# Splitting the row threshold into three f16 parts: subtractions on TensorE instead of VectorE

## The chip, the cores and the metric

The kernel runs on one core of a Trainium2 chip. The metric is the device time of one execution in microseconds (us), as the median over several runs. Engines are TensorE (PE, its weight loads apart as PEld), VectorE (DVE), ScalarE (ACT), GpSimd (POOL) and SyncE (SP, which here issues DMAs).

## What is computed

Masked attention over 8 batches of 8 heads, then a mixture of experts that takes one expert for each token:

```python
scores = scale * np.matmul(q, k.transpose(0, 1, 3, 2))          # q, k, v: (8, 8, 576, 64)
thresh = np.max(scores, axis=-1, keepdims=True) - tau
scores = np.where(scores >= thresh, scores, -1000000000.0)
scores = scores - np.max(scores, axis=-1, keepdims=True)
attn = np.exp(scores)
attn = attn / (np.sum(attn, axis=-1, keepdims=True) + 1e-09)
x = np.matmul(attn, v)                  # then laid out as (4608, 512)
logits = x @ w_gate                     # 8 experts
expert_idx = np.argmax(logits, axis=1)
...
    h = np.maximum(xe @ w1[e], 0.0)     # w1[e]: 512 x 1024
    ye = h @ w2[e]
    out[mask] = gate_w[mask, None] * ye
```

## The kernel before

The kernel treats the heads as 32 pairs. Queries, keys, values and weights are held as two f16 parts (high and low), so that products in f16 reach the accuracy that is wanted. A pair takes eleven steps, and each step works on one tile of up to 128 x 512 scores.

Each pair goes through the scores twice. The first pass (`s_unit`, L312 and L314 on TensorE) computes scores `s` with queries as rows, and VectorE takes the negated maximum of each row (`nm`, L324). The second pass (`st_unit`, L360 and L361) computes them again transposed (`st`), with the threshold already subtracted: the rows 64 to 66 of the tile `CQ` hold, for each query, minus its row's maximum plus a multiple of tau, and the product L361 adds them to the scores by three rows of ones. ScalarE then takes the exponential (`e`, L377), VectorE zeroes what lies below the threshold (`e`, L380), ScalarE rounds to f16 (`ph`, L385) and GpSimd makes the rest (`pl`, L386). TensorE multiplies both with the values (`av`, L422 to L424). The first pass runs ten steps ahead of the second.

Since `CQ` is f16, the threshold is split into three f16 parts. This is `parts`: VectorE takes the minimum of the two halves of the row maxima (`r`, L331), TensorE transposes it (`pst`, L335) into 9 x 128 elements of a PSUM tile, and then a chain of four operations makes the three parts `ptT`: ScalarE rounds value plus threshold (L340), VectorE subtracts the rounded part from value plus threshold and writes the rest beside it in PSUM (`y`, L341), ScalarE rounds the rest (L342), VectorE subtracts again and writes the third part as f16 (L343). Three DMAs on SyncE's queue bring the parts into `CQ` (`rows`, L348).

The helper `chain` spreads such operations over steps: element i of a list goes to the step k + i // 2, alternately to the middle and to the end of a step. The PSUM tile of `pst` comes from a pool of one buffer with the tag `m`, which the logits (`lg`, L494), the ranks (`rk`, L539 to L542) and the counts use as well. 

Other work between: a high part of queries and keys (`hi`, ScalarE L230) is multiplied by a unit matrix into PSUM (`hi`, TensorE L244), and VectorE makes the low part from it (`lo`, L245). The values go the same way (`vop` on ScalarE L276, `hi_v` on TensorE L244, `vop` on VectorE L245). When a batch is done (four pairs), its logits, its choice of experts and the ranks of its tokens are computed, and GpSimd scatters the tokens' rows to DRAM by expert (L560, `xs`), after it scaled them (`xn`, L465). Towards the end of attention the experts' weights are loaded (`wf`, L717) and split into two f16 parts (`wb`, ScalarE L730 and VectorE L731); tokens are gathered (L764), transposed by DMA (L774 for gathered tokens, L480 for those of the logits) and multiplied (`h`, L819, and `y`, L852). Two of the first token slots lie in a tile `spare`.

The order on each engine isn't the order of the code alone: the framework builds the program with its own list scheduler, which orders all instructions by a model of their times. An edit at one place can so move instructions at others.

Of the kernel before, what the change touches and what calls it, by code (L numbers as in the profile page):

```python
# [9 lines left out]
F16 = mybir.dt.float16  # L10
# [3 lines left out]
AF = mybir.ActivationFunctionType  # L14
ALU = mybir.AluOpType
AX = mybir.AxisListType

P = 128
# [32 lines left out]
def kernel(  # L51
# [9 lines left out]
    nc = tc.nc  # L61

    cpool = ctx.enter_context(tc.tile_pool(name="cpool", bufs=1))
# [19 lines left out]
    ident = cpool.tile([P, P], F32, name="ident")  # L83
    make_identity(nc, ident)
    ident_h = cpool.tile([P, P], F16, name="ident_h")
    nc.gpsimd.tensor_copy(ident_h, ident)
    ones = cpool.tile([P, P], F16, name="ones")
    nc.gpsimd.memset(ones, 1.0)
    before = cpool.tile([P, P], F16, name="before")
# [3 lines left out]
    thr = cpool.tile([P, 1], F32, name="thr")  # L93
# [95 lines left out]
    def after(k, f, where=END):  # L189
        plan(now[0] + k, f, where)  # L190

    def chain(k, fs, at_once=False):

        if at_once:
            for f in fs:
                after(k, f, END)
            return
        for i, f in enumerate(fs):
            i += slot[0] > FRONT and k == 0
            after(k + i // 2, f, END if i % 2 else MID)  # L200
# [125 lines left out]
    def parts(n):  # L326


        nm = st[n]["nm"]
        r = small.tile([P, 9], F32, tag="r", name=f"r_{n}")  # L330
        nc.vector.tensor_reduce(r, nm.rearrange("p a t -> p t a"), axis=AX.X, op=ALU.min)  # L331

        def turn():
            ps = ps_m.tile([P, 512], F32, tag="m", name=f"pst_{n}")
            nc.tensor.transpose(ps[0:9, 0:P], r, ident)  # L335
            x, y = ps[0:9, 0:P], ps[0:9, P:2 * P]
            t = small.tile([9, 3, P], F16, tag="ptT", name=f"ptT_{n}", bufs=1)
            v, a = nc.vector, nc.scalar
            chain(1, [
                lambda: a.activation(t[:, 0], x, AF.Identity, bias=thr[0:9]),  # L340
                lambda: v.scalar_tensor_tensor(y, x, thr[0:9], t[:, 0], ALU.add, ALU.subtract),  # L341
                lambda: a.copy(t[:, 1], y),  # L342
                lambda: (v.tensor_tensor(t[:, 2], y, t[:, 1], ALU.subtract), rows(t)),  # L343
            ])

        def rows(t):
            for p in range(3):
                nc.sync.dma_start(  # L348
                    st[n]["CQ"][64 + p:65 + p].rearrange("p (t c) -> p t c", t=9), t[:, p]
                )  # L350

        after(1, turn)
# [714 lines left out]
    if True:  # L1067
# [9 lines left out]
        while busy:  # L1077
# [3 lines left out]
            for z in (("st", "s"), ("s", "st"))[TUNE["ord"]]:  # L1081
                n, t = divmod(k + (NSTEP + LEAD if z == "s" else 0), NSTEP)
# [11 lines left out]
            n, t = divmod(k - TUNE["av"], NSTEP)  # L1094
# [95 lines left out]
```

## Time and profile before

| | |
|---|---|
| median of three runs | 1040.5 us (1040.37 to 1044.72) |
| the profiled execution | 1042.02 us |
| its span (first to last instruction) | 1040.3 us |
| mean granted clock of TensorE | 0.976 |
| TensorE busy | 958.2 us, 92% |
| VectorE busy | 719.1 us, 69% |
| ScalarE busy | 653.1 us, 63% |
| GpSimd busy | 556.3 us, 53% |

A row of the profile names a line of the kernel, an engine, an operation and, after it, the tile that it writes and those that it reads; "x32" is a count, and a time in brackets with an arrow is the idle time of the engine just before and what ended it. Attention fills the span to about 620 us, the experts the rest; pairs begin every 16 to 17 us, but for six that take about 22.

### The profile page before, as it was taken

Reading aid. Unit: us, or ns where it says so; the run is one execution under the profiler, and the core shown is the slowest. Engines: PE = TensorE matmul, PEld = TensorE weight load, DVE = VectorE, ACT = ScalarE, POOL = GpSimd, SP = SyncE. Lnnn points to the kernel's source line nnn. Section 1 sums busy time; section 2 is a strip of 40 time slices with the busy share of each in tenths; the row PEclk is TensorE's granted clock in tenths of the full one; section 3 lists DMA queues with packets and bytes.
Section 4 is the critical chain, followed back from the end, with each engine's and each line's share of the span. In section 5 each row is a group of like instructions: output and inputs, shape, how many; then the busy total and the mean of one; then the engine's idle time right before and its main releaser. Section 6 shows DMA issues by size and latency. Waiting matters only on the chain.

```text
span 1040.3 us, 28272 instructions
## 1 busy us (share of the span) xinstructions
PE 958.2 (92%) x11336; PEld 622.9 (60%) x11336; DVE 719.1 (69%) x1443; ACT 653.1 (63%) x1098; POOL 556.3 (53%) x460
## 2 busy tenths in 40 slices
PE   2799998999898998998996689999999999999996
PEld 1365655566464665564663476767766676667683
DVE  6999998899797997997998964664332433423650
ACT  2588998888787987987977773524342433433641
POOL 3266887976977967968867773153221222122121
PEclk9999999899999999999998898999999999999998
DMA  6534554754465645546534536989746746556720
GB/s 185 140 92 110 138 131 116 164 122 116 132 156 144 134 102 155 139 105 180 127 87 134 140 84 214 310 266 236 231 142 172 232 132 178 170 156 217 225 82 25
DMA packets 142562, 159.16 MB, mean 153 GB/s; under 512 B 96345, under 2 KB 112731, under 8 KB 142428
## 3 DMA queue, kind: packets, MB, share of 16 engines
q1 hardware_dynamic: 126796, 100.35, 37.7%
q10 hardware_dynamic: 6480, 27.53, 8.9%
q0 software_dynamic: 9152, 29.45, 8.7%
q8 instruction: 90, 1.47, 0.6%
q14 instruction: 44, 0.36, 0.1%
HBM read 90.24 MB, written 19.44 MB: 105 GB/s over the span
## 4 chain that ended last, share of the span: by engine, by line
PE 50%; DVE 7%; issue 6%; DMA 4%; ACT 3%; POOL 1%; another core or an unknown queue 1%; POOLq 0%; ACTq 0%; DVEq 0%; SPq 0%
PE h L819 16%; PE y L852 14%; PE st L360 3%; PE s L312 3%; PE s L314 3%; PE st L361 3%; PE av L422 2%; DMA out_dram<-o,gt 2%; DVE wb L731 2%; PE av L423 2%; PE av L424 2%; DVE e L380 2%; DVE nm L324 1%; DMA wf<-in_w_dram 1%
## 5 line engine op out<-in xcount | busy, mean ns | idle before, releaser
L386 POOL TENSOR_TENSOR pl<-e,ph 128x1024 f16<-128x1024 f32 x158 | 336.8, 2142 | 144.2 <-ACT ph L385 103.2
L377 ACT ACTIVATE e<-st,ntau 128x512 f32<-128x512 f32 (+1 forms) x352 | 223.1, 653 | 65.5 <-PE st L361 36.2
L324 DVE TENSOR_REDUCE nm<-s 128x1 f32<-128x512 f32 x320 | 200.4, 633 | 39.9 <-PE s L314 26.0
L380 DVE SCALAR_TENSOR_TENSOR e<-st,e 128x512 f32<-128x512 f32 (+1 forms) x352 | 219.8, 635 | 5.4 <-ACT e L377 4.6
L852 PE MATMUL y<-wb,hl 128*128 128x512 f16 (+1 forms) x1056 | 203.6, 362 | 1.1 <-issue 0.7
L819 PEld LDWEIGHTS <-wb 128*128 128x128 f16 x2304 | 190.4, 99 | 23.3 <-issue 4.9
L819 PE MATMUL h<-xTm,wb 128*128 128x256 f16 (+2 forms) x2112 | 198.0, 255 | 3.1 <-issue 3.1
L422 PE MATMUL av<-vop,ph 128*128 128x65 f16 (+1 forms) x1536 | 186.3, 195 | 4.7 <-issue 2.5
L424 PE MATMUL av<-vop,ph 128*128 128x64 f16 (+1 forms) x1536 | 185.7, 196 | 2.3 <-issue 2.3
L423 PE MATMUL av<-vop,pl 128*128 128x65 f16 (+1 forms) x1536 | 184.8, 194 | 3.2 <-issue 2.9
L385 ACT CAST ph<-e 128x1024 f16<-128x1024 f32 x160 | 166.8, 1043 | 18.6 <-DVE e L380 18.3
L422 PEld LDWEIGHTS <-ph 128*128 128x128 f16 (+1 forms) x1536 | 148.8, 101 | 31.5 <-issue 11.9
L423 PEld LDWEIGHTS <-pl 128*128 128x128 f16 (+1 forms) x1536 | 148.6, 100 | 29.1 <-issue 12.3
L312 PE MATMUL s<-QK 128*128 128x512 f16 (+3 forms) x640 | 141.4, 299 | 24.7 <-DMA QK<-lo 17.3
L424 PEld LDWEIGHTS <-ph 128*128 128x128 f16 (+1 forms) x1536 | 148.7, 100 | 24.7 <-issue 11.5
L731 DVE SCALAR_TENSOR_TENSOR wb<-wf,wb 128x1024 f16<-128x1024 f32 x96 | 125.2, 1341 | 49.1 <-ACT wb L730 45.7
L852 PEld LDWEIGHTS <-hl 128*128 128x128 f16 (+1 forms) x1056 | 94.5, 100 | 101.3 <-issue 6.3
L360 PE MATMUL st<-QK 128*128 128x512 f16 (+3 forms) x640 | 142.4, 298 | 8.8 <-DVE e L380 5.3
L361 PE MATMUL st<-CQ,ck 128*128 128x512 f16 (+3 forms) x640 | 139.7, 293 | 0.7 <-DMA CQ<-hi 0.4
L314 PE MATMUL s<-ck,CQ 128*128 128x512 f16 (+3 forms) x640 | 137.8, 292 | 1.2 <-DMA CQ<-hi 1.2
L864 POOL DMA_INDIRECT out_dram<-o,gt x40 | 44.4, 1111 | 143.9 <-ACT o L863 127.1
L807 ACT ACTIVATE hl<-h 128x512 f16<-128x512 f32 (+1 forms) x80 | 45.8, 573 | 113.6 <-PE h L819 106.7
(182 smaller groups left out, 1092.8 us busy)
## 6 DMA issues: line engine op xcount, KB each, us to landing
wf<-in_w_dram SPq DMA_DIRECT2D x96, 512.0 KB
qkf<-in_qk_dram ACTq DMA_DIRECT2D x30, 576.0 KB
vf<-in_v_dram ACTq DMA_DIRECT2D x15, 640.0 KB
QK<-hi SPq DMA_DIRECT2D x64, 144.0 KB
QK<-hi SPq DMA_DIRECT2D x64, 72.0 KB
QK<-lo SPq DMA_DIRECT2D x64, 72.0 KB
ck<-lo SPq DMA_DIRECT2D x64, 72.0 KB
CQ<-hi SPq DMA_DIRECT2D x64, 64.0 KB
```

Of the source, the lines that this page charges most:

```text
L312: nc.tensor.matmul(sc[rows, oc], d["QA"][a][:, cols], d["KB"][a][:, CH[c]], start=True, stop=False)
L324: nc.vector.tensor_reduce(o, sc[:, 0:width(t)], axis=AX.X, op=ALU.max, negate=True)
L360: nc.tensor.matmul(sc[rows, oc], d["KB"][a][:, cols], d["QA"][a][:, CH[c]], start=True, stop=False)
L361: nc.tensor.matmul(sc[rows, oc], d["CK"][a][:, cols], d["CQ"][:, q], start=False, stop=True)
L377: nc.scalar.activation(pf, sc, AF.Exp, bias=ntau, scale=0.125 / SS)
L380: nc.vector.scalar_tensor_tensor(pf, sc, 0.0, pf, ALU.is_ge, ALU.mult)
L386: (nc.vector if (n, t) in PLV else nc.gpsimd).tensor_tensor(l, pd, h, ALU.subtract)
L422: nc.tensor.matmul(av, h, vop[:, tv, 0:W], start=i in (0, NT) and m == 0, stop=False)
L423: nc.tensor.matmul(av, l, vop[:, tv, 0:W], start=False, stop=False)
L424: nc.tensor.matmul(av[:, 0:D], h, vop[:, tv, W:W + D], start=False, stop=last)
L819: nc.tensor.matmul(o, Wt[:, c, wh, f], x, start=c == 0 and z == 0, stop=c == 3 and z == 2,)
L852: nc.tensor.matmul(o, h[:, hh], Wt[:, f, wh, c], start=f == 0 and z == 0, stop=f == 7 and z == 2)
```

## The change

A constant `minus` (9 x 9, f16, minus the unit matrix) is made once. The rest `y` is no longer written beside the value. Instead TensorE subtracts the rounded part from the value in PSUM: a product of `minus` and the part, accumulated on what `pst` left there. ScalarE makes all three parts with the same operation, which adds the threshold and rounds. The chain has five elements now instead of four.

```diff
+    minus = cpool.tile([9, 9], F16, name="minus")
+    nc.vector.tensor_scalar(minus, ident[0:9, 0:9], -1.0, None, ALU.mult)
...
-            nc.tensor.transpose(ps[0:9, 0:P], r, ident)
-            x, y = ps[0:9, 0:P], ps[0:9, P:2 * P]
+            nc.tensor.matmul(ps[0:9, 0:P], r, ident, start=True, stop=True, is_transpose=True)
+            x = ps[0:9, 0:P]
             t = small.tile([9, 3, P], F16, tag="ptT", name=f"ptT_{n}", bufs=1)
-            v, a = nc.vector, nc.scalar
+
+            def part(p):
+                nc.scalar.activation(t[:, p], x, AF.Identity, bias=thr[0:9])
+
+            def less(p):
+                nc.tensor.matmul(x, minus, t[:, p], start=False, stop=True, skip_group_check=True)
+
             chain(1, [
-                lambda: a.activation(t[:, 0], x, AF.Identity, bias=thr[0:9]),
-                lambda: v.scalar_tensor_tensor(y, x, thr[0:9], t[:, 0], ALU.add, ALU.subtract),
-                lambda: a.copy(t[:, 1], y),
-                lambda: (v.tensor_tensor(t[:, 2], y, t[:, 1], ALU.subtract), rows(t)),
+                lambda: part(0), lambda: less(0), lambda: part(1), lambda: less(1), lambda: (part(2), rows(t)),
             ])
```

In the changed kernel the roundings have the line L343, the subtractions L346, `pst` L337; lines further down are higher by six.

The scheduler orders the changed program anew. Three places follow; names carry the pair, then the tile where there is one, then a running number, so `st_20_3` is tile 3 of pair 20.

The first place is the chain of pair 21. TensorE before:

```order
L244 MATMUL hi_23_2_8198<-hi_23_8145,ident_h_99 128x384
L335 MATMUL pst_21_8150<-ident_94,r_21_8127 9x128
L422 LDWEIGHTS ph_19_8_7800
L422 MATMUL av_19_1_8391<-vop_1_166,ph_19_8_7800 128x65
L423 LDWEIGHTS pl_19_8_7801
L423 MATMUL av_19_1_8391<-vop_1_166,pl_19_8_7801 128x65
L424 LDWEIGHTS ph_19_8_7800
L424 MATMUL av_19_1_8391<-vop_1_166,ph_19_8_7800 128x64
```

TensorE in the changed kernel, at the same place:

```order
L246 MATMUL hi_23_2_8221<-hi_23_8168,ident_h_99 128x384
L337 MATMUL pst_21_8173<-ident_94,r_21_8150 9x128
L430 LDWEIGHTS ph_19_8_7819
L430 MATMUL av_19_0_8197<-vop_1_168,ph_19_8_7819 64x64
L346 LDWEIGHTS minus_101
L346 MATMUL pst_21_8173<-ptT_21_8175,minus_101 9x128
L246 LDWEIGHTS ident_h_99
L246 MATMUL hi_v10_1_0_8225<-vop_0_167,ident_h_99 128x320
```

One product stands between `pst` and the first subtraction, and a `hi_v` product, which needs `vop`, follows at once; before, products of `av` followed `pst`. ScalarE at this place before:

```order
L377 ACTIVATE e_20_2_8156<-st_20_3_8190,ntau_107 128x512
L430 COPY x_4_7117<-av_19_0_8174 128x4x65
L431 COPY xh_4_7116<-av_19_0_8174 64x65
L526 COPY was_4_9422<-run_151 128x8
L340 ACTIVATE ptT_21_8152<-pst_21_8150,thr_105 9x128
L276 ACTIVATE vop_0_165<-vf_10_7535 128x10x64
L211 DMA qkf_25_8538<-in_qk_dram 128x1152
L342 CAST ptT_21_8152<-pst_21_8150 9x128
L385 CAST ph_20_2_8157<-e_20_2_8156 128x1024
```

ScalarE in the changed kernel:

```order
L532 COPY was_4_9445<-run_153 128x8
L383 ACTIVATE e_20_2_8179<-st_20_3_8213,ntau_109 128x512
L343 ACTIVATE ptT_21_8175<-pst_21_8173,thr_107 9x128
L278 ACTIVATE vop_0_167<-vf_10_7557 128x10x64
L436 COPY x_4_7138<-av_19_0_8197 128x4x65
L437 COPY xh_4_7137<-av_19_0_8197 64x65
L343 ACTIVATE ptT_21_8175<-pst_21_8173,thr_107 9x128
L213 DMA qkf_25_8562<-in_qk_dram 128x1152
```

The first part and `vop` now stand ahead of the copies `x` and `xh`, and the second part behind them.

The second place is GpSimd's scatter of batch 3 (`xs`, five of them in one row), in pair 20. Before:

```order
L386 TENSOR_TENSOR plc_20_10_8306<-e_20_10_8304,phc_20_10_8305 128x64
L386 TENSOR_TENSOR pl_20_8_8260<-e_20_8_8258,ph_20_8_8259 128x1024
L560 DMA xs_81<-R_197,posi_3_7978 36864x514 x5
L465 TENSOR_TENSOR xn_4_0_8576<-x_4_7117,rs_4_8520 128x512
L465 TENSOR_TENSOR xn_4_1_8755<-x_4_7117,rs_4_8520 128x512
L386 TENSOR_TENSOR pl_20_4_8381<-e_20_4_8379,ph_20_4_8380 128x1024
L386 TENSOR_TENSOR pl_20_6_8438<-e_20_6_8436,ph_20_6_8437 128x1024
```

In the changed kernel:

```order
L392 TENSOR_TENSOR plc_20_10_8330<-e_20_10_8328,phc_20_10_8329 128x64
L392 TENSOR_TENSOR pl_20_8_8280<-e_20_8_8278,ph_20_8_8279 128x1024
L392 TENSOR_TENSOR pl_20_4_8405<-e_20_4_8403,ph_20_4_8404 128x1024
L566 DMA xs_81<-R_199,posi_3_8001 36864x514 x5
L471 TENSOR_TENSOR xn_4_0_8600<-x_4_7138,rs_4_8544 128x512
L471 TENSOR_TENSOR xn_4_1_8780<-x_4_7138,rs_4_8544 128x512
L392 TENSOR_TENSOR pl_20_6_8462<-e_20_6_8460,ph_20_6_8461 128x1024
```

One `pl` has moved ahead of the scatters.

The third place is SyncE's queue where the experts begin (`xTg` and `xTm` are transposed tokens, `wf` weights). Before:

```order
L717 DMA wf_2_0_0_13271<-in_w12_dram 128x1024
L774 DMA_TRANSPOSE spare_13173<-spare_13173 128x8x128
L717 DMA wf_2_1_0_13314<-in_w12_dram 128x1024
L717 DMA wf_1_3_0_13347<-in_w12_dram 128x1024
L717 DMA wf_2_0_1_13363<-in_w12_dram 128x1024
L480 DMA_TRANSPOSE xTg_7_0_13226<-R_197 128x8x128
L774 DMA_TRANSPOSE spare_13173<-spare_13173 128x8x128
L480 DMA_TRANSPOSE xTg_7_0_13226<-R_197 128x8x128
```

In the changed kernel, where five loads and a transpose stand between `wf_2_0_0` and the first row here:

```order
L486 DMA_TRANSPOSE xTg_7_0_13260<-R_199 128x8x128
L723 DMA wf_2_1_1_13578<-in_w12_dram 128x1024
L723 DMA wf_1_1_1_13589<-in_w12_dram 128x1024
L486 DMA_TRANSPOSE xTg_7_2_13279<-R_199 128x8x128
L723 DMA wf_2_3_0_13593<-in_w12_dram 128x1024
L486 DMA_TRANSPOSE xTg_7_2_13279<-R_199 128x8x128
L486 DMA_TRANSPOSE xTg_7_4_13290<-R_199 128x8x128
L780 DMA_TRANSPOSE spare_13207<-spare_13207 128x8x128
```

Both transposes of `spare` now come behind those of the last batch's tokens.

## The prediction

> **What bounds the kernel now.** I read the page first (its chain of waits, by engine), then cut the attention part into stretches by the view of windows, and then asked in each stretch which engine waits for which.
>
> ```profile
> PE 50%; DVE 7%; issue 6%; DMA 4%; ACT 3%; POOL 1%; another core or an unknown queue 1%; POOLq 0%; ACTq 0%; DVEq 0%; SPq 0%
> ```
>
> TensorE has half of the chain that ended last, VectorE 7%. That is a mean over stages, so the next view is one of stages: the start, four plain pairs (9 to 12), the pair that begins at 403.8, the last two pairs with the first weight splits, and a window of the MoE part. Behind a stretch and its length stand the busy us (and instructions) of TensorE, its weight loads, VectorE, ScalarE and POOL, then TensorE's granted clock.
>
> ```profile
> 26.00:51.20 25.20, 19.66 (x129) 8.23 (x130) 23.18 (x48) 13.09 (x23) 5.17 (x4) 0.93 0.52 142
> 191.20:257.00 65.80, 65.29 (x985) 40.57 (x983) 61.71 (x134) 56.36 (x104) 49.48 (x32) 1.00 0.55 125
> 403.80:426.10 22.30, 18.95 (x236) 11.07 (x235) 16.78 (x34) 16.39 (x29) 20.53 (x17) 0.92 0.42 128
> 549.00:600.00 51.00, 32.83 (x431) 20.85 (x431) 46.10 (x69) 35.78 (x58) 38.35 (x28) 0.87 0.49 128
> 640.00:660.00 20.00, 20.00 (x239) 14.29 (x238) 11.51 (x15) 10.73 (x16) 8.59 (x8) 0.96 1.11 292
> ```
>
> In the four plain pairs both TensorE (65.29 of 65.8 us) and VectorE (61.71) look full, so busy time can't decide; the waits can. First TensorE's and VectorE's in 191.2 to 257, then TensorE's in 549 to 600 (us in total, times, longest):
>
> ```profile
> PE pst L335 <- DVE r L331: 0.4, 1, 0.4
> DVE nm L324 <- PE s L314: 2.9, 8, 0.7
> PE st L360 <- DVE e L380: 5.0, 2, 2.7
> PE s L312 <- DVE e L380: 4.3, 1, 4.3
> ```
>
> In plain pairs TensorE waits for nothing but once 0.4 us, while VectorE waits eight times for TensorE: **TensorE is the bound there**, VectorE a close second with 65.8 − 61.7 = 4.1 us to spare in four pairs. At the end of attention it is the other way round, TensorE waits over 9 us for VectorE. In the pair at 403.8 POOL is the fullest, and TensorE has 3.4 us idle. In the MoE part TensorE is full again, and the change has no instruction there.
>
> **The change part by part.** The tile views give each operation's minimum, median and maximum in ns:
>
> ```profile
> L340 ACT ACTIVATE ptT<-pst,thr x32: 342/354/359, 29.6 to 585.6; 9x128 f16<-9x128 f32 x32
> L341 DVE SCALAR_TENSOR_TENSOR pst<-pst,thr,ptT x32: 337/341/347, 32.0 to 591.0; 9x128 f32<-9x128 f32 x32
> L342 ACT CAST ptT<-pst x32: 233/250/256, 32.4 to 592.0; 9x128 f16<-9x128 f32 x32
> L343 DVE TENSOR_TENSOR ptT<-pst,ptT x32: 268/269/279, 32.7 to 593.5; 9x128 f16<-9x128 f32 x32
> ```
>
> *VectorE.* 32 × (341 + 269) = 19.5 us go, 0.61 in a pair. In plain pairs this lies beside a full TensorE and is worth nothing. It is worth something where TensorE waits for VectorE: chains 29 to 31 in the last stretch, whose 46.1 busy us fill most of 51, 2 × 0.61 = 1.2 us there (the third chain's share falls into VectorE's wait for weights). And at the start:
>
> ```profile
> 32.40 0.26 ACT L342 CAST ptT<-pst 9x128 f16<-9x128 f32 x1 [2.42 <-DVE pst L341]
> 32.56 0.74 ACT L276 ACTIVATE vop<-vf 128x640 f16<-128x640 f32 x1
> ...
> 33.36 0.44 PE L244 MATMUL hi_v<-vop,ident_h 128*128 128x320 f16 x2 [3.77 <-ACT vop L276]
> ```
>
> L341 stands behind VectorE's queue there, ScalarE waits 2.42 us for it with `vop` behind, and TensorE waits 3.77 us for `vop`. Without VectorE in the chain this 2.42 goes; late next are VectorE's own low parts and maxima (23.18 busy of 25.2), so I count 1.4 (between 0.61, one chain's work, and 2.42). Together −2.6 (bounds 0 and −19.5).
>
> *ScalarE.* 32 more roundings of 354 ns, and 32 × (354 − 250) for the ones that were casts: 14.7 us, 0.46 in a pair. The cover is its slack: 65.8 − 56.4 = 9.4 us in four pairs, 2.4 in one. Counted as nothing; with the cover gone it would be 14.7.
>
> *TensorE.* 64 products of 9x128. No such row exists; the nearest are the 512-column products, which start 0.21 apart, and `pst` itself, the same 128 columns in f32, whose follower starts 0.11 later (the last row is for the waits below):
>
> ```profile
> 210.78 0.28 PE L335 MATMUL pst<-ident,r 128*9 128x128 f32 x1 [0.38 <-DVE r L331]
> 210.89 0.19 PE L423 MATMUL av<-vop,pl 128*128 128x65 f16 x1
> ...
> 212.00 0.38 PE L360 MATMUL st<-QK 128*128 128x512 f16 x1
> 212.21 0.38 PE L361 MATMUL st<-CQ,ck 128*128 128x512 f16 x1
> 212.25 0.36 ACT L340 ACTIVATE ptT<-pst,thr 9x128 f16<-9x128 f32 x1
> ```
>
> A quarter of 0.21 is 0.054: 64 × 0.054 = 3.5 us, or 7.0 by the other row. Below, nothing, if they all fall into waits that are there anyway. I take 3.5, since the new products are f16 like the 512-column ones.
>
> *New waits on TensorE.* Each first subtraction waits for ScalarE's first part, each second one for the second, and behind them in TensorE's order stand products of other pairs that need neither. The order puts from 0 to 3.9 us of other products between `pst` and the first subtraction, and 1.2 to 3.8 between the two. That is enough in most pairs: ScalarE's part 0 followed `pst` by 1.47 us and took 0.36 in pair 11, where 2.1 us of products now stand between. In pair 21 hardly one product is left between them, and the `hi_v` products follow directly:
>
> ```profile
> 393.17 0.27 PE L335 MATMUL pst<-ident,r 128*9 128x128 f32 x1
> ...
> 393.49 0.36 ACT L340 ACTIVATE ptT<-pst,thr 9x128 f16<-9x128 f32 x1
> ...
> 393.75 0.73 ACT L276 ACTIVATE vop<-vf 128x640 f16<-128x640 f32 x1
> ```
>
> Part 0 ends at 393.85, `vop` at 394.48, and TensorE has only till about 393.3 to do: 0.6 us of wait for the subtraction, then some 0.7 for `hi_v`, 1.3 in all. The same arithmetic with each pair's rows gives 0.4 to 2.0 us in eight more pairs and almost nothing in the others, 7.7 in sum. Pairs 9, 17 and 25 cost nothing: TensorE waits there for `vop` anyway, behind the same L340.
>
> ```profile
> PE hi_v L244 <- ACT vop L276: 3.3, 3, 1.5
> PE hi_v L244 <- ACT ptT L340: 3.0, 1, 3.0
> ```
>
> Three of the waits (pairs 14, 21, 29: 2.9 us) lie close ahead of or in a stretch where TensorE idles for POOL. So I take 5. Bounds: 0, if these waits are all taken back there, and 13, if in each of the 26 pairs without a long idle time the rounding's 0.36 us and the two hand-overs around it (0.5) stand open.
>
> *`m` and the rows.* The one buffer of `m` is held until the last rounding, a half step longer; its next users are the logits and ranks, several steps on. The three row transfers leave a half step later, seven steps before `st` of that pair reads them. I count nothing: a late transfer would show as a wait of L361 for `CQ`, and the lists of waits above have none.
>
> *POOL's order.* In the pair at 403.8 five scatters, the last of them the first row here, and two `xn` stand ahead of `pl`:
>
> ```profile
> 409.68 0.96 POOL L560 DMA_INDIRECT xs<-R,posi  x1 [0.30 <-issue]
> 410.67 2.04 POOL L465 TENSOR_TENSOR xn<-x,rs 128x512 f32<-128x512 f32 x2
> 412.67 2.12 POOL L386 TENSOR_TENSOR pl<-e,ph 128x1024 f16<-128x1024 f32 x1
> ```
>
> In three such blocks one `pl` now stands ahead of the scatters or of the two `xn`. That can shorten TensorE's idle time by up to one `pl` (2.1) each, −6, or only move it; it can also push the scatters back, +2. I take −1.
>
> *Start of the MoE part.* On SyncE the transposes of the two spare slots move behind some nine more transfers and transposes, and TensorE takes other products first. TensorE is full there now (20.00 of 20.0 us from 640), and its products on the spare slots run from 653.4:
>
> ```profile
> L819 PE MATMUL h<-spare,wb x192: 216/219/220, 653.4 to 670.2; 128*128 128x128 f16 x192
> L774 SPq DMA_TRANSPOSE spare<-spare x2: 2587/2934/3282, 637.4 to 645.3; - x2
> ```
>
> A second transpose at 645.3 with nine entries more ahead (0.7 to 3 us each) comes some 13 us later, and other products have to fill that. I take +1; bounds +6, if only half of these 13 us find other products, and −3, if the other order fills waits that stand ahead of 640.
>
> **The sum.** The profiled execution took 1042.0 us (span 1040.3 and 1.7 around it): 1042.0 + 3.5 + 5 − 2.6 − 1 + 1 = 1047.9. It lies 1.5 above the median of the three runs, so on their scale 1046.4, rounded 1046.5, which is 0.6% slower.
>
> **Rivals.** *A, VectorE is the bound.* For it: 61.71 of 65.8 us busy, and the end and start wait for it. Against: it waits for TensorE 2.9 us in four pairs, TensorE for it 0.4. If each pair shortened by its 0.61: 1040.5 − 19.5 = 1021, with the subtractions up to 1031. The Trainium skill, Perfetto Trace Analysis, section Identifying the Most-Contended Engine, says that a matmul's busy share misjudges TensorE and that the engine with the highest occupancy is to be relieved first. By that rule VectorE (94% of these pairs against 62% for weight loads) would be the one, and this rival true. The waits of this trace speak against it.
>
> *B, the order comes out better.* Six pairs of the trace are as long as that at 403.8, 22.3 us instead of 65.8 / 4 = 16.5, so some 34 us are there to be had. If the three POOL blocks give 2.1 each, the waits nothing, and the rest is as above: 1042.0 + 3.5 − 2.6 − 6.3 + 1 − 1.5 = 1036, with a spread of 1030 to 1041. For it: the rows of the order. Against: POOL has 20.53 of 22.3 us to do in that pair whatever the order.
>
> *C, slower: the new waits halve the clock.* After idle times of TensorE the granted clock falls to a half for 3.4 us:
>
> ```profile
> 324.80:326.40 1.60, 0.08 (x2) 0.04 (x1) 0.35 (x1) 1.52 (x7) 1.60 (x1) 1.00 0.79 287
> 327.75:331.20 3.45, 3.45 (x27) 1.92 (x27) 2.29 (x5) 0.78 (x2) 2.54 (x4) 0.51 0.77 226
> 469.70:471.20 1.50, 0.02 (x1) 0.02 (x1) 0.35 (x1) 1.45 (x6) 1.35 (x2) 1.00 0.92 290
> 471.20:475.00 3.80, 3.68 (x35) 1.65 (x35) 2.89 (x8) 2.26 (x6) 2.89 (x4) 1.00 0.61 167
> ```
>
> An idle time of 1.5 us was followed by a half clock once and once not. The place is the first subtraction in pairs 3, 5, 15, 21 and 29, with `hi_v` behind it; the price is 1.7 us for each half-clock stretch, and it decides from idle times of about 1.5 us, which my 2.0 for pair 15 and 1.3 for pair 21 touch. All five, with the waits in full: 1042.0 + 3.5 + 7.7 + 8.5 − 2.6 − 1.5 = 1057.6; range 1052 to 1062. The Trainium skill, TensorE: Matmul & The Clock Gate, section HAM oscillation, puts the limit at idle gaps of about 3.4 us; by that no new wait would halve the clock and C would fall. The row at 327.75, behind 1.5 us, doesn't agree with a limit on one gap alone, so C keeps its chance.
>
> That the change doesn't do what it says is small: the order has the two subtractions and three roundings in each pair.
>
> **How the numbers follow.** Forecast 0.60 (1041 to 1053), A 0.10, B 0.15, C 0.15. The bound of about 0.5% (5.2 us, what a measurement of this kernel tells from no change) lies at 1035.3 and 1045.7. Faster: A and two thirds of B, 0.20. Same: the rest of B and 0.27 of the forecast, 0.32. Slower: 0.33 of the forecast and C, 0.48. The range 1032 to 1058 leaves out A and about half of C.
>
> **What would show it.** Right: 96 roundings of about 354 ns on ScalarE; plain pairs 0.1 to 0.5 us longer, with TensorE still full and VectorE 0.6 less busy in each; TensorE's list of waits with new entries for `pst` behind ScalarE of some 5 us in sum; the idle time at 29.6 shorter by 1 to 2 us. Wrong: plain pairs shorter by 0.3 or more (A); long pairs at 404 and 549 shorter by 2 (B); new stretches at a clock of 0.5 in plain pairs (C); subtractions more than 0.11 us apart from their followers; or TensorE waiting between 640 and 670.

## The result and the profile after

The changed kernel takes 1051.6 us (median of 5 runs, 1047.2 to 1054.0) beside 1041.2 of the kernel before in the same comparison: ratio 1.0085, 95% interval 1.0056 to 1.0115. It is slower, by more than the forecast 0.6% (1046.5 us) and inside the range. The profiled execution took 1047.2 us with a span of 1045.5, the fastest of the five; so the traces, 5.2 us apart, account for a part of the difference of medians only. A second comparison, on a chip where the kernel before takes 1028 us, gave 1.0061 (1.0043 to 1.0080). All comparisons are by ratio, since chips differ: the kernel before took 1041, 1045, 1028 and 1045 us in the four of this study.

First the page's chain of waits of the changed kernel, shares of the span by engine:

```profile
PE 38%; DMA 6%; issue 5%; DVE 3%; POOL 1%; ACT 1%; SPq 0%; POOLq 0%; ACTq 0%; DVEq 0%
```

VectorE's share falls from 7 to 3%, as one would wish, and the time rises. Then the view of tiles, for `ptT` and for `minus` (duration in ns: minimum, median, maximum):

```profile
L343 ACT ACTIVATE ptT<-pst,thr x96: 337/354/360, 30.5 to 597.0; 9x128 f16<-9x128 f32 x96
L346 PE MATMUL pst<-ptT,minus x64: 211/217/267, 30.9 to 595.1; 9*9 9x128 f16 x64
L346 PEld LDWEIGHTS <-minus x64: 79/79/83, 30.4 to 595.1; 9*9 9x9 f16 x64
```

The change does what it says: 96 roundings of 354 ns on ScalarE and 64 subtractions on TensorE. Their 217 ns are no price, since products overlap; their price is the distance between starts, below.

The windows of before that answer to stages, and the same stages after (start to the first `st` of pair 1; pairs 9 to 12; pairs 29 and 30; the rest). The columns are those of the prediction's windows. First before:

```profile
0.00:51.20 51.20, 27.05 (x173) 11.33 (x174) 40.60 (x100) 18.35 (x30) 13.53 (x48) 0.97 0.59 164
191.20:258.30 67.10, 66.59 (x1006) 41.38 (x1004) 62.92 (x137) 57.66 (x108) 50.78 (x32) 1.00 0.54 123
548.70:599.90 51.20, 33.02 (x431) 20.78 (x430) 46.30 (x70) 35.86 (x59) 38.65 (x28) 0.87 0.49 129
599.90:1040.30 440.40, 423.21 (x3808) 300.07 (x3806) 187.90 (x329) 177.92 (x252) 119.74 (x140) 0.98 0.61 181
```

After:

```profile
0.00:48.40 48.40, 26.38 (x177) 11.19 (x178) 38.41 (x96) 18.57 (x31) 13.01 (x48) 1.00 0.62 173
190.50:259.60 69.10, 68.18 (x1013) 41.81 (x1012) 63.45 (x128) 61.03 (x113) 51.97 (x32) 1.00 0.54 122
554.70:605.00 50.30, 37.65 (x508) 24.25 (x507) 44.89 (x77) 39.30 (x69) 40.29 (x31) 0.83 0.58 146
605.00:1045.50 440.50, 418.65 (x3738) 296.08 (x3735) 182.91 (x315) 175.83 (x245) 120.77 (x138) 0.98 0.62 179
```

VectorE is no less busy in the second window than before, since the longer window holds one `e` and one `nm` more; over the whole span it falls from 719.1 us to 704.0. The start is 2.8 us shorter, the last two pairs 0.9, the experts' part the same to 0.1. The four plain pairs are 2.0 us longer, 0.5 each, with TensorE as full as before. I read each pair's start (its first L361, L367 after) from both traces and added up: the 23 plain pairs (1 to 28 without the long ones 8, 13, 16, 21 and 24) take 386.5 us before and 397.3 after, **+10.8**; the five long ones 111.0 and 109.1, −1.9. So −2.8 + 10.8 − 1.9 − 0.9 + 0.1 = +5.3, the two traces' difference to rounding. In these two traces all of the loss is in plain pairs.

Is it waiting? The list of TensorE's waits after the change, in pairs 1 to 7 and in pairs 9 to 12:

```profile
PE st L367 <- DMA CQ<-ptT: 1.0, 1, 1.0
PE st L366 <- DVE nm L326: 0.3, 1, 0.3
...
PE pst L337 <- DVE r L333: 0.6, 1, 0.6
PE st L366 <- DVE nm L326: 0.2, 1, 0.2
```

Of the subtractions (`pst L346`) there is no wait at all in these eleven pairs. In all 23, TensorE's idle times sum to 5.4 us before and 6.9 after: 0.3 of it at a subtraction (in pair 20), 0.8 at two `hi_v` products behind `vop`, and the 1.0 of the first row above, where `st` waits for the parts in `CQ`. But for those 0.3, the waits that the list of the whole run has at L346 (10.4 us in sum) lie at the start and in the long pairs, which idled before as well. So here are the rows around one subtraction that waits for nothing:

```profile
249.89 0.20 PE L428 MATMUL av<-vop,ph 128*128 128x65 f16 x1
249.92 0.20 PE L429 MATMUL av<-vop,pl 128*128 128x65 f16 x1
249.96 0.19 PE L430 MATMUL av<-vop,ph 128*128 128x64 f16 x1
250.08 0.22 PE L346 MATMUL pst<-ptT,minus 9*9 9x128 f16 x1
250.23 0.20 PE L428 MATMUL av<-vop,ph 128*128 128x65 f16 x1
250.27 0.20 PE L429 MATMUL av<-vop,pl 128*128 128x65 f16 x1
```

Between `av` products starts lie 0.03 us apart. The subtraction starts 0.12 behind its forerunner and its follower 0.15 behind it. From 249.96 to 250.23 are 0.27 us where 0.03 would stand without it: **0.24 us for one subtraction**, not the 0.054 that its columns ask. Some 0.09 comes ahead of it and 0.09 behind. Behind 512-column products it is the same (starts 0.31 apart ahead instead of 0.215). 64 x 0.24 is 15.4 us; 46 of them, those of the 23 plain pairs, are 11.0, and 10.8 were measured. That the two come so close is luck in part, since 1.5 of the 10.8 are idle time. Added up from start to start, without the idle times, the plain pairs take 381.1 us before and 390.4 after, 9.2 more.

### The profile page after: what moved, and what is told of

The parts are those of the page before. It is cut to its first block, busy times and chain, and to the rows that moved or that the text cites. A ratio compares the mean times of both kernels' runs of the same rounds, so it can differ in the third digit from the quotient of the medians.

```text
span 1045.5 us, 28318 instructions
## 1 busy us (share of the span) xinstructions
PE 964.5 (92%) x11400; PEld 625.6 (60%) x11400; DVE 704.0 (67%) x1380; ACT 668.1 (64%) x1130; POOL 560.1 (54%) x460
## 4 chain that ended last, share of the span: by engine, by line
PE 38%; DMA 6%; issue 5%; DVE 3%; POOL 1%; ACT 1%; SPq 0%; POOLq 0%; ACTq 0%; DVEq 0%
PE h L825 17%; PE y L858 13%; DMA out_dram<-o,gt 3%; DMA wf<-in_w_dram 2%; PE st L366 1%; PE st L367 1%; PE av L428 1%; PE s L314 1%; DVE wb L737 1%; PE av L429 1%; PE av L430 1%; PE s L316 1%; DVE nm L326 1%; DVE e L386 1%; POOL out_dram L870 0%
## 5 line engine op out<-in xcount | busy, mean ns | idle before, releaser
L825 PE MATMUL h<-xTm,wb 128*128 128x256 f16 (+2 forms) x2112 | 195.9, 254 | 1.5 <-DMA xTm<-Rm 1.5
L428 PE MATMUL av<-vop,ph 128*128 128x65 f16 (+1 forms) x1536 | 183.5, 194 | 2.2 <-ACT xh L437 1.0
L430 PE MATMUL av<-vop,ph 128*128 128x64 f16 (+1 forms) x1536 | 182.4, 195 | 1.6 <-issue 1.6
L429 PE MATMUL av<-vop,pl 128*128 128x65 f16 (+1 forms) x1536 | 182.4, 194 | 0.6 <-issue 0.5
L737 DVE SCALAR_TENSOR_TENSOR wb<-wf,wb 128x1024 f16<-128x1024 f32 x96 | 121.5, 1301 | 55.6 <-ACT wb L736 51.0
L367 PE MATMUL st<-CQ,ck 128*128 128x512 f16 (+3 forms) x640 | 138.6, 291 | 1.4 <-DMA CQ<-ptT 1.0
L736 ACT ACTIVATE wb<-wf 128x1024 f16<-128x1024 f32 x96 | 97.8, 1050 | 31.0 <-DMA wf<-in_w_dram 13.5
```

The costliest lines, as they stand in the source:

```text
L428: nc.tensor.matmul(av, h, vop[:, tv, 0:W], start=i in (0, NT) and m == 0, stop=False)
L429: nc.tensor.matmul(av, l, vop[:, tv, 0:W], start=False, stop=False)
L430: nc.tensor.matmul(av[:, 0:D], h, vop[:, tv, W:W + D], start=False, stop=last)
L825: nc.tensor.matmul(o, Wt[:, c, wh, f], x, start=c == 0 and z == 0, stop=c == 3 and z == 2,)
```

## The experiments

Theory A: the subtraction's own price, set by the shape of its weights. Theory B: TensorE waits for ScalarE's parts. Theory C, later O: the scheduler's order of other work. Theory R, of the last runs: what full weights gain comes from VectorE's relief at the start and in the last two pairs.

**128 rows of weights** (9 columns as before):

```diff
-    minus = cpool.tile([9, 9], F16, name="minus")
-    nc.vector.tensor_scalar(minus, ident[0:9, 0:9], -1.0, None, ALU.mult)
+    minus = cpool.tile([P, 9], F16, name="minus")
+    nc.vector.memset(minus, 0.0)
+    nc.vector.tensor_scalar(minus[0:9], ident[0:9, 0:9], -1.0, None, ALU.mult)
+    ptT = cpool.tile([P, 3, P], F16, name="ptT")
+    nc.vector.memset(ptT, 0.0)
...
-            t = small.tile([9, 3, P], F16, tag="ptT", name=f"ptT_{n}", bufs=1)
+            t = ptT[0:9]
...
-                nc.tensor.matmul(x, minus, t[:, p], start=False, stop=True, skip_group_check=True)
+                nc.tensor.matmul(x, minus, ptT[:, p], start=False, stop=True, skip_group_check=True)
```

> The changed kernel, but the subtraction's unit matrix is 128 x 9 instead of 9 x 9 (rows beyond 9 are zero) and the parts lie in a constant tile of 128 rows (the rest zero), so that the weights have the height of all other products. Theory A (own price: in the trace a 9x9 product takes 0.24 us of TensorE, since the products before and behind it each stand 0.09 us further off than their size asks; 64 of them are 15.4 us): the spacing falls to about 0.06 us and the time by about 12 us, to 1040 (ratio to the kernel before 0.995 to 1.003). Theory B (TensorE waits for ScalarE's parts): nothing changes, ratio 1.007 to 1.010. Theory C (the scheduler's new order of other work costs the time): 1.004 to 1.012, since the order is a third one.

Measured: 1.0038 (1.0015 to 1.0062). That is less than B expected, and the gain that A expected isn't there. The rows say why; TensorE in this run:

```profile
211.28 0.19 PE L433 MATMUL av<-vop,ph 128*128 128x64 f16 x1
211.40 0.22 PE L349 MATMUL pst<-ptT,minus 128*9 128x128 f16 x1
211.56 0.20 PE L431 MATMUL av<-vop,ph 128*128 128x65 f16 x1
```

0.12 and 0.16 again: full height alone doesn't take the charge away. Why the ratio is below the changed kernel's all the same isn't shown; the order is another one, and the chip may be.

**No subtraction**, parts 1 and 2 zero (the threshold keeps its first part only):

```diff
-                nc.scalar.activation(t[:, p], x, AF.Identity, bias=thr[0:9])
+                nc.scalar.activation(t[:, p], x, AF.Identity, bias=zero if p else thr[0:9], scale=0.0 if p else 1.0)
...
-                nc.tensor.matmul(x, minus, t[:, p], start=False, stop=True, skip_group_check=True)
+                pass
```

> The changed kernel without the subtractions on TensorE; parts 1 and 2 are written as zeros by the same roundings on ScalarE, so the threshold is left with its first f16 part only. A and B both take their loss away: 15 us under the changed kernel, ratio to the kernel before 0.992 to 0.998 (what the relief of VectorE is worth, less ScalarE's work). C: the ratio stays above 1.004.

Measured: 1.0008 (0.9986 to 1.0030), where A and B expected a gain; once more on another chip:

> The run without subtractions (parts 1 and 2 zero) again, on the same chip as the run with 128-column subtractions. Theory A and R alone: it does less than that one, so its ratio is 0.983 to 0.992. Theory O: near its first ratio, 0.998 to 1.003, above the kernel that does more.

Measured: 1.0016 (0.9989 to 1.0042). Without the subtractions the loss is gone, which A and B both say. But both expected it to be faster than before, and it isn't. Whether ScalarE's added work eats up VectorE's relief or the order does (O) isn't separated. The two profiles lose 6 to 9 us behind the last pair, where nothing of the chain is left. (With the shorter threshold tokens may also be spread otherwise over the experts; the number of expert products is the same.) And plain pairs take 392.5 and 391.5 us without any subtraction, 5 to 6 more than in the trace of before: 2 to 3 of it are idle time, 3 lie between starts. The kernel before was profiled in the first comparison only, so whether the chip or the order makes this is open, and the 10.8 above can't all be put down to the subtractions with certainty.

**64 more products beside VectorE's operations of the kernel before:**

```diff
+            def extra(i):
+                nc.tensor.matmul(ps[0:9, (2 + i) * P:(3 + i) * P], minus, ident_h[0:9], start=True, stop=True)
...
-                lambda: v.scalar_tensor_tensor(y, x, thr[0:9], t[:, 0], ALU.add, ALU.subtract),
+                lambda: (v.scalar_tensor_tensor(y, x, thr[0:9], t[:, 0], ALU.add, ALU.subtract), extra(0)),
...
-                lambda: (v.tensor_tensor(t[:, 2], y, t[:, 1], ALU.subtract), rows(t)),
+                lambda: (v.tensor_tensor(t[:, 2], y, t[:, 1], ALU.subtract), rows(t), extra(1)),
```

> The kernel before with 64 more products of 9x128 with a 9 x 9 unit matrix, two in each chain, beside the two VectorE operations, into unused columns of the same PSUM tile; they read constants only and nothing reads them. A: 64 x 0.24 where TensorE is full, ratio 1.010 to 1.015. B: only their columns count, 3.5 us, ratio 1.002 to 1.005. C: anything up to 1.01, with a spacing of 0.06 around the products.

Measured: 1.0376 (1.0340 to 1.0412), far from all. The products weren't free of waits as I meant: the framework lets a product into a PSUM tile wait for VectorE's write to another part of that tile (`pst L343 <- DVE pst L347`, 16.5 us in 8 waits). The run doesn't tell A from B. It shows that a small product can make far longer waits than its own price; these waits are 16.5 of some 39 us, and the rest isn't taken apart.

**Subtractions a step later:**

```diff
-                lambda: part(0), lambda: less(0), lambda: part(1), lambda: less(1), lambda: (part(2), rows(t)),
+                lambda: part(0), wait, wait, lambda: less(0), lambda: part(1), wait, wait, lambda: less(1), lambda: (part(2), rows(t)),
```

with `wait` an empty element.

> The changed kernel with each subtraction planned a step later behind the rounding that it needs (two empty elements in the chain). A: no change, ratio 1.006 to 1.011. B: the waits for the parts go (about 6 us of the trace's waits at the first and second subtraction), ratio 1.001 to 1.005. C: undecided.

Measured: 1.0185 (1.0148 to 1.0221), against B, and worse than A expected too. TensorE's waits from 53 to 540 us:

```profile
PE pst L346 <- ACT ptT L343: 10.0, 3, 4.7
PE st L368 <- DMA CQ<-ptT: 4.0, 6, 1.5
```

The parts now reach `CQ` late, and `st` waits for them, six times; and where the subtraction waits for its part it waits longer (4.7 us at most, 0.9 in the changed kernel). The chain has less to spare than the seven steps that I had read from the code.

**Only the shape**, in the kernel before: 62 products that wait for nothing, behind the copies `hi`, with 9 x 9 weights and then with 128 x 128:

```diff
         nc.tensor.matmul(y, ident_h, hi, start=True, stop=True)
+        if nm[0] != "v" and nm[-1] != "2":
+            nc.tensor.matmul(sc[0:9, 384:512], minus, ident_h[0:9], start=True, stop=True)
...
         nc.tensor.matmul(y, ident_h, hi, start=True, stop=True)
+        if nm[0] != "v" and nm[-1] != "2":
+            nc.tensor.matmul(sc[:, 384:512], ident_h, ident_h, start=True, stop=True)
```

> The kernel before with one more product of 9x128 with a 9 x 9 unit matrix behind the first two of the three products of each pair that copy the high part of queries and keys into PSUM (62 in all), into unused columns of the same tile; it reads constants and waits for nothing. A: 62 x 0.24 = 15 us, 13 of it in pairs where TensorE is full: ratio 1.010 to 1.014. B: 62 x 0.054 = 3.3 us: ratio 1.002 to 1.004.

> As the run before, but the additional products have the whole 128 x 128 unit matrix as weights, so only the shape differs. A: 62 x 0.054 = 3.3 us, ratio 1.002 to 1.004, and 0.06 us a product in the trace. If it is the number of products and not their shape, the ratio is that of the run with 9 x 9.

Measured: 1.0129 (1.0107 to 1.0151) and 1.0036 (1.0018 to 1.0054), both where A has them. TensorE with 9 x 9 weights:

```profile
199.64 0.33 PE L246 MATMUL hi<-hi,ident_h 128*128 128x384 f16 x1
199.90 0.22 PE L248 MATMUL hi<-ident_h,minus 9*9 9x128 f16 x1
200.05 0.20 PE L428 MATMUL av<-vop,ph 128*128 128x64 f16 x1
```

and with 128 x 128:

```profile
195.52 0.33 PE L244 MATMUL hi<-hi,ident_h 128*128 128x384 f16 x1
195.68 0.22 PE L246 MATMUL hi<-ident_h 128*128 128x128 f16 x1
195.73 0.19 PE L426 MATMUL av<-vop,ph 128*128 128x64 f16 x1
```

The same forerunner, the same moving columns, the same follower: 0.41 us from `hi` to `av` in the one, 0.21 in the other. The 9 x 9 product is charged 0.1 ahead and 0.1 behind, the full one nothing but its columns, 0.05 to 0.06. No wait is in it. 62 x 0.19 is 11.8 us, and the ratios lie 0.0093 apart, 9.6 us of 1028. This pair of runs, on one chip and with equal numbers of products, shows the price of the shape most cleanly.

**Full weights in the changed kernel**, with a product that clears the tile's other rows:

```diff
-    minus = cpool.tile([9, 9], F16, name="minus")
-    nc.vector.tensor_scalar(minus, ident[0:9, 0:9], -1.0, None, ALU.mult)
+    minus = cpool.tile([P, P], F16, name="minus")
+    nc.vector.tensor_scalar(minus, ident, -1.0, None, ALU.mult)
+    ptT = cpool.tile([P, 3, P], F16, name="ptT")
+    nc.vector.memset(ptT, 0.0)
...
+            nc.tensor.matmul(ps[:, 0:P], ptT[64:P, 0], ident_h[64:P], start=True, stop=True)
             nc.tensor.matmul(ps[0:9, 0:P], r, ident, start=True, stop=True, is_transpose=True)
...
-                nc.tensor.matmul(x, minus, t[:, p], start=False, stop=True, skip_group_check=True)
+                nc.tensor.matmul(ps[:, 0:P], minus, ptT[:, p], start=False, stop=True, skip_group_check=True)
```

> The changed kernel, but the subtraction's weights are minus the whole 128 x 128 unit matrix and the parts lie in a constant tile of 128 rows (zero beyond 9), so that the product has as many columns of weights as its neighbours; a product with zero weights ahead of each transposition clears the other rows of the PSUM tile. Theory A, in its second form (the price is for the change from 128 columns of weights to 9 and back, as the 128 x 9 weights of the first try left the spacing at 0.125 ahead and 0.154 behind): 0.19 us less for each subtraction, 64 x 0.19 = 12 us under the changed kernel, less 2 us for the clearing products: ratio 0.997 to 1.001. Theory B (waits for ScalarE): as the changed kernel, 1.006 to 1.011.

with the changed kernel beside it on the same chip:

> The changed kernel once more, as the reference for the runs of this call, since the kernel before took 4 us more in the last call than in the first. Both theories: ratio 1.006 to 1.011.

Measured: 0.9904 (0.9876 to 0.9932), and 1.0061 (1.0043 to 1.0080) for the reference: 1.6% between the two. TensorE:

```profile
209.71 0.19 PE L432 MATMUL av<-vop,pl 128*128 128x65 f16 x1
209.74 0.22 PE L349 MATMUL pst<-ptT,minus 128*128 128x128 f16 x1
209.80 0.19 PE L433 MATMUL av<-vop,ph 128*128 128x64 f16 x1
```

0.03 and 0.06: nothing is charged any more. Plain pairs fall from 401.3 us in the changed kernel's trace on this chip to 390.0; 4.3 of these 11.3 us are idle time, 7.0 lie between starts. The kernel beats the one before here, by more than A expected (0.997 to 1.001). The charge can't be all of that: the two traces also differ by 5.3 us in the long pairs and by 6.5 behind the last pair, where there are no subtractions. Whether the gain holds on another chip:

> The kernel with subtraction weights of 128 columns once more, as the reference of this call, whatever the chip. Ratio 0.986 to 0.995; if the gain of the last call was one of that chip alone, nearer to 1.

Measured: 0.9980 (0.9956 to 1.0004), outside the expected 0.986 to 0.995. So it is no slower than before on either chip, and 1.0% faster on one of the two. On the chip of the gain the five long pairs took 94.5 to 99.8 us in all four kernels profiled, on the others 109 to 126; why is open.

**Rows or columns?** Weights of 9 rows and 128 columns, again with a product that clears the tile's other rows:

```diff
+    minus = cpool.tile([9, P], F16, name="minus")
+    nc.vector.tensor_scalar(minus, ident[0:9], -1.0, None, ALU.mult)
...
+                nc.tensor.matmul(ps[:, 0:P], minus, t[:, p], start=False, stop=True, skip_group_check=True)
```

> The changed kernel with weights of 9 rows and 128 columns (the negated unit matrix in the first nine columns) and parts of 9 rows, and the clearing product. If only the columns of the weights make the price (as the first try with 128 rows and 9 columns suggests), the spacing is 0.054 with nothing ahead and behind, and the ratio that of the 128 x 128 weights, 0.986 to 0.995. If rows count as well: spacing as in the changed kernel, ratio 1.004 to 1.011.

Measured: 1.0047 (1.0026 to 1.0068), and TensorE:

```profile
214.85 0.19 PE L433 MATMUL av<-vop,pl 128*128 128x65 f16 x1
214.98 0.23 PE L350 MATMUL pst<-ptT,minus 9*128 9x128 f16 x1
215.14 0.20 PE L434 MATMUL av<-vop,ph 128*128 128x64 f16 x1
```

0.13 and 0.16. Rows are charged as columns are: 9 x 9, 128 x 9 and 9 x 128 all cost about 0.24 us among 128 x 128 neighbours.

Traces taken on one chip can be set side by side, plain pairs from start to start and without idle times: on one, 393.7 us with 9 rows against 386.9 with full weights and 384.2 with no subtraction; on another, 393.4 in the changed kernel against 386.4 with full weights, and 391.4 with the added 9 x 9 products against 386.3 with the full ones. The shape so costs 5 to 7 us there. 46 x 0.19 would be 8.7; which other distances shrink in exchange isn't shown.

**VectorE's old load on top of the full weights:**

```diff
+            def spend():
+                nc.vector.scalar_tensor_tensor(
+                    idle, ident[0:9], thr[0:9], ident_h[0:9], ALU.add, ALU.subtract
+                )
...
-                lambda: part(0), lambda: less(0), lambda: part(1), lambda: less(1), lambda: (part(2), rows(t)),
+                lambda: part(0), lambda: (less(0), spend()), lambda: part(1), lambda: (less(1), spend()),
+                lambda: (part(2), rows(t)),
```

> The same kernel with two more operations on VectorE in each chain, of the form of the removed L341 (9x128, sum and difference), on constants and into a tile that nothing reads, so VectorE has its old load again while TensorE and ScalarE have that of the run before. Theory R (what 128-column subtractions gain over the kernel before comes from VectorE's relief in the stretches that VectorE bounds, the start and the last two pairs): most of it goes, ratio 0.996 to 1.004. Theory O (it comes from the order that the scheduler happened to make): no change, ratio 0.987 to 0.995.

Measured: 1.0161 (1.0129 to 1.0194), beyond both. The view of tiles tells why it can't decide:

```profile
L353 DVE SCALAR_TENSOR_TENSOR idle<-ident,thr,ident_h x64: 241/333/2310, 13.5 to 140.7; 9x128 f16<-9x128 f32 x64
```

Since these operations wait for nothing, the scheduler put all 64 ahead of 141 us: 38 us of work before pair 6 begins at 152. Pairs 1 to 5 take 97.8 us there, 83.0 in the kernel before. So VectorE is near to being the bound in plain pairs; R and O are not told apart by this run. For O speaks that the run without subtractions, which does less than the one with full weights, isn't faster on the same chip (1.0016 beside 0.9980).

## Why the prediction was right, and which term was mis-sized

*What bounds the kernel.* Right. Plain pairs follow TensorE's starts, and VectorE's 0.6 us less did not shorten them. Rival A (VectorE the bound, 1021 to 1031) fell; the run without subtractions is its clean case, and its plain pairs take 391.5 to 392.5 us, not less than 386.5. Whether ScalarE's 0.5 us more costs anything isn't separated from the order by any run. Rival B (the order better, 1030 to 1041) fell too: its sign came at 404, where pair 21 is 2.3 us shorter, but the five long pairs give 1.9 in sum and the last two 0.9.

*TensorE's work.* Mechanism right, size wrong: 3.5 us forecast, 7.0 at most, 15.4 by the rows measured (0.24 each), 11.0 of it in the 23 plain pairs. The prediction's own sign of being wrong came here: subtractions stand 0.15 us from their followers, more than 0.11. The step that failed is the choice of row: "I take 3.5, since the new products are f16 like the 512-column ones." Those have full weights. The trace of before has rows of the right kind, which I didn't use, products with 64-column weights between full ones (TensorE's timeline, kernel before):

```profile
251.75 0.19 PE L424 MATMUL av<-vop,ph 128*128 128x64 f16 x1
251.87 0.22 PE L422 MATMUL av<-vop,phc 128*64 128x65 f16 x1
251.93 0.20 PE L423 MATMUL av<-vop,plc 128*64 128x65 f16 x1
252.05 0.20 PE L360 MATMUL st<-QK 128*128 128x64 f16 x1
```

The first of them starts 0.12 behind a full one, and the next full one 0.12 behind the second, where full products of this size stand 0.03 apart. Products of this same shape in a row aren't charged (kernel before):

```profile
177.84 0.20 PE L422 MATMUL av<-vop,ph 128*64 128x65 f16 x1
177.87 0.19 PE L423 MATMUL av<-vop,pl 128*64 128x65 f16 x1
177.90 0.20 PE L424 MATMUL av<-vop,ph 128*64 128x64 f16 x1
```

By these rows the charge goes with the change from one shape of weights to another, and a single subtraction pays it twice; no experiment puts two subtractions next to one another. The row of `pst` misled as well: its f32 weights are 128 x 9, and its distance from its forerunner is 0.03.

*New waits on TensorE.* Forecast 5, bounds 0 and 13. In plain pairs 0.3 us came at a subtraction and 0.8 at `hi_v`. The long waits at a subtraction (2.3, 3.0, 0.9 and 3.0 us, at 181, 272, 328 and 476) lie in long pairs, which in sum got 1.9 shorter. My estimate set the distance from `pst` to L340 in the trace of before against the new order; ScalarE's order had moved with it. So a term of +5 that came to about 1 in plain pairs, and a term that was 11.9 too small by the rows (8.5 in plain pairs), made a sum that was about right: 5.9 forecast for the profiled execution, 5.2 measured. That is luck.

*`m` and the rows.* Counted as nothing; `st` waited once for the parts in `CQ`, 1.0 us at 117.5.

*VectorE's relief.* Forecast −2.6 (start −1.4, end −1.2); in the traces −2.8 and −0.9. At the start TensorE waits 1.08 us for `vop` instead of 3.77, plus 0.45 at each subtraction. Over eight profiles without VectorE in the chain (all but the ones with later subtractions and with the added load, 53.2 and 54.1 us) pair 1 begins at 47.5 to 50.0 us, over four with it at 51.2 to 53.1: the ranges don't meet, so this relief is real. How much of it is VectorE's own time isn't separated: behind the wait of 3.77 the granted clock fell to a half for 3.4 us, behind the shorter waits of the changed kernel's trace it didn't (0.97 and 1.00 in the windows of the start), which can be up to 1.7 of the 2.8.

*POOL's order and the experts' start.* Forecast −1 and +1; the long pairs gave −1.9, the rest +0.1. The +0.1 is a balance and not a sign that nothing happened. TensorE did wait between 640 and 670, which the prediction had named as a sign of being wrong: 7.4 us in 3 waits of `lg` for the last batch's tokens, not there before, and only 0.4 for the spare slots that the prediction had in mind. Against that, the time ahead of 640 is filled better, first before, then after:

```profile
599.90:640.00 40.10, 35.49 (x617) 29.79 (x616) 19.07 (x59) 19.54 (x42) 23.24 (x19) 0.89 0.34 101
605.00:640.00 35.00, 34.55 (x632) 28.99 (x630) 22.64 (x53) 22.27 (x42) 21.07 (x14) 1.00 0.53 163
```

More products are done in 35.0 us than before in 40.1, at full clock. That the two effects cancel is chance.

*Rival C.* No half-clock stretch arose in plain pairs: the granted clock is 1.00 in all of them, as in 190.5 to 259.6. The clock did fall behind the long waits at subtractions in pairs 8 and 13 (at 182 and 274), but before had a fall in these pairs as well (at 181 and 266). It also fell behind the wait of 3.0 us in pair 24, where before had none; that pair is 2.2 us longer. The window of the changed kernel:

```profile
475.00:478.40 3.40, 1.95 (x8) 0.46 (x8) 1.00 (x3) 2.24 (x8) 3.10 (x2) 0.54 0.60 217
```

The clock stands behind the five engines, 0.54 there; in its place pair 21 lost the half-clock stretch that it had before, and is 2.3 shorter. As a mechanism C is right at one place, in sum it fell. That the median was 10 us up and not 5, as the profiled runs were, is open. The order of the scheduler is the same in all five runs, but the granted clock isn't: it is 0.977 and 0.979 in the two fastest (1047.2 and 1049.7 us) and 0.970 to 0.973 in the other three. Where these lose it no profile shows, so C may have a part in it.

## What to carry to other kernels

A small product among full ones isn't priced by its moving columns: look for a product with small weights among full ones in the trace, and read the distance between starts ahead of it and behind it, since busy time and idle time both hide the charge. Padding both dimensions of its weights to those of its neighbours takes the charge away; here that turned a loss of 0.6% into a gain of 1.0% on one chip, and gave no clear difference from before (0.9980) on another, where weights of 9 rows lost 0.5%. And an extra instruction for a test should hang on what the tested one hangs on, or a list scheduler may move it to another place, as it did with VectorE's added load.

## What the runs showed of the hardware

An f16 product with 9 rows of weights, 9 columns, or both starts about 0.09 us later behind a full one, and the full one behind it about 0.09 later again (0.12 and 0.15 measured where 0.03 and 0.054 stand otherwise). With 64 columns of weights it is 0.12 ahead and 0.12 behind, and 0.03 among products of this shape. The transposition `pst`, whose weights are 128 x 9 in f32, starts 0.03 behind a full one, so the charge ahead isn't made for every small shape.

The load of the weights doesn't explain it: 79 ns for 9 x 9, 84 for 128 x 9, 90 for 9 x 128, about 97 for full ones. The Trainium skill, TensorE: Matmul & The Clock Gate, section LDWEIGHTS (loading the stationary operand), says that a load's time goes by columns alone and not by rows. That rows matter little the traces roughly confirm (90 against 97 ns); by columns they don't, since 9 columns take 79 to 84 ns and 64 columns 110, more than the 97 of 128. What part of the engine makes the charge isn't shown by any run.
